# More q, k and x transposes by DMA, loads moved up, and a last output tile of 384 + 128 columns

## The chip, the cores and the metric

The kernel runs on one core of one Trainium2 chip. Time is device time in microseconds (us) for one execution; lower is better. Each kernel was run several times, alternating with the kernel before on the same chip. Most executions of a kernel agree well; a run over 1.5% above the fastest of the same kernel is called slow and left out of the ratios, though not of the medians.

Ratios are the mean time of one kernel's fast runs over the mean of the other's fast runs in the same rounds, so they are not quite the ratios of the medians that stand beside them. Where I turn a difference of ratios into microseconds I multiply by 249.3.

## The reference

Sliding-window attention with four sink keys, then a gated feed-forward layer on its output:

```python
scores = q @ k.T / sqrt(64)                     # 4 batches, 8 heads, 768 positions
keep   = (key position < 4) | (0 <= rel < 128)  # four sinks, a window of 128
a      = softmax(where(keep, scores, -1e9))
x      = (a @ v), heads side by side            # 3072 tokens x 512
xn     = x / sqrt(mean(x * x) + 1e-6) * rms_g
g      = xn @ w_gate                            # 512 x 1536
out    = (g * sigmoid(g) * (xn @ w_val)) @ w_out
```

## The kernel before

The 3072 tokens are 24 blocks of 128: `g = 6 b + t`, batch `b`, block `t` of the batch. Four blocks make a feed-forward group of 512 columns, so there are six groups, G = 0 to 5. Attention of later blocks is laid into the "slots" between the feed-forward parts of earlier groups.

A block's q and k are loaded as bf16 with the tokens on the partitions, and must be transposed before scores can be taken. The kernel does this on TensorE up to block 13 and for block 18, else by DMA on SyncE's queue:

```python
DMA_T_FROM = 14          # q, k: from this block by DMA
DMA_X_FROM = 12          # x: the same

def by_dma(g):
    return g >= DMA_T_FROM and g % NT > 0          # NT = 6: not the first block of a batch

def unit_t(g):
    ...
    if by_dma(g):
        for i, src in enumerate((QS.pop(g), KS_.pop(g))):
            nc.sync.dma_start_transpose(out=QKT[b][:, i, :, t * P:(t + 1) * P], in_=...)
        return
    ps = psum.tile(...)                            # 8 transposes on TensorE,
    transposes(ps, QS.pop(g), 0)
    transposes(ps, KS_.pop(g), HP * P)
    nc.scalar.copy(out=QKT[b]..., in_=ps...)       # and one copy by ScalarE
```

The four sink keys of a batch are the first four columns of its first block's k. They are copied out once per batch, by two small copies on ScalarE:

```python
def unit_sink(b):
    ks = sink.tile([P, HP * KSW], BF16, name="ksk")
    ...
    for hi in range(2):
        nc.scalar.copy(out=ksv[pr, :, hi * NS:(hi + 1) * NS], in_=QKT[b][pr, 1, :, 0:NS])
    ...
```

GpSimd issues the loads and, from block 8 on, also masks the exponentials. Output tiles go through three buffers (`opool`, bufs=3), copied out of PSUM by ScalarE and stored from SyncE's queue:

```python
slots:  step(g) puts unit_s(g), unit_attend(g - 1), unit_t(g + 2 or g + 3), unit_sink, two loads
LOADS = [(14, 15), (16, 17), (18, 19), (20, 21), (22, 23)]     # one pair per step, from g = 9
```

All PSUM tiles are one bank each and take eight banks in turn.

The softmax here doesn't subtract the row's maximum and nothing guards it: scores larger than these inputs give would overflow.

## Time and profile before

| | before |
|---|---|
| median of three runs | 249.14 us (249.09 to 249.48) |
| span of the profiled run | 248.5 us |
| TensorE busy, granted clock | 241.8 us, 1.00 |
| q, k transposes on TensorE | 15 blocks of 24 |
| x transposes on TensorE | 12 blocks of 24 |
| DMA engines | full for 19 of 40 slices, until about 118 us, then mostly idle |

TensorE is the bound: a kernel can only be shorter if TensorE does less, or waits less at the two ends. The lines that show it are in the prediction. Some words used there and below: the chain is the sequence of instructions and transfers that ended last, followed back from the last instruction; the pitch is the time from one instruction's start to the next one's. Tile names: `pqk` and `pxt` are transposes on TensorE, `qkT` and `xnt` the transposed q, k and x; `pT` are scores, `et` their exponentials, `pv` their products with v; `pg` and `pvl` are the gate and value matmuls, `th` the tanh of the gate, `p` and `hT` what VectorE makes of them; `po` is the output matmul and `osb` its copy.

### The profile page before, as it was taken

What the parts mean: (1) busy time and instruction counts of PE and PEld (TensorE: products, weight loads), DVE (VectorE), ACT (ScalarE), POOL (GpSimd) and SP (SyncE); (2) the same over time, 40 slices, a digit from 0 to 9 for tenths busy, and PEclk for the clock granted to TensorE, in tenths of its full rate; (3) what the DMA queues carried; (4) which work ended last, traced back from release to release, by engine and by line L of the source; (5) the groups of instructions that cost most, each with busy time, mean ns of one, the idle gap of its engine ahead of it and who ended that gap; (6) DMA issues with size and microseconds to landing.
All of it is one profiled execution on the core that took longest, in us unless ns stands there. A gap on an engine that the chain in (4) does not pass through costs nothing.

```text
span 248.5 us, 4926 instructions
## 1 busy us (share of the span) xinstructions
PE 241.8 (97%) x1850; PEld 129.5 (52%) x1850; DVE 163.6 (66%) x368; ACT 145.2 (58%) x336; POOL 105.1 (42%) x141
## 2 busy tenths in 40 slices
PE   7999999999999999999999999999999999999994
PEld 2566887856445554544454454444444444444443
DVE  5465896878467789339778368769167885387700
ACT  2779657898977774874674375674475242333221
POOL 8977676496398995970331000233231000000000
PEclk9999999999999999999999999999999999999999
DMA  9999999999959999599000694001610003500022
GB/s 128 153 171 192 190 160 187 183 155 188 126 69 144 148 129 161 91 161 164 0 3 12 158 168 88 0 4 22 190 46 0 3 0 63 190 3 0 0 86 84
DMA packets 102873, 24.96 MB, mean 100 GB/s; under 512 B 91841, under 2 KB 99905, under 8 KB 102850
## 3 DMA queue, kind: packets, MB, share of 16 engines
q0 software_dynamic: 80704, 13.90, 73.4%
q1 hardware_dynamic: 20962, 10.43, 18.4%
q10 hardware_dynamic: 1184, 0.33, 0.6%
q8 instruction: 14, 0.23, 0.4%
q14 instruction: 9, 0.07, 0.1%
HBM read 28.31 MB, written 6.29 MB: 139 GB/s over the span
## 4 chain that ended last, share of the span: by engine, by line
PE 90%; ACT 4%; DVE 2%; DMA 2%; issue 0%; ACTq 0%
PE pg L642 25%; PE pvl L642 25%; PE po L712 22%; PE pT L411 4%; PE pv L467 3%; PE pqk L245 2%; PE pv L471 2%; DMA osb<-in_q_dram 2%; ACT et L420 2%; PE pw L332 1%; PE po L684 1%; PE pT L342 1%; PE pv L453 1%; ACT sq L519 1%; PE pT L357 1%; PE pxt L612 1%
## 5 line engine op out<-in xcount | busy, mean ns | idle before, releaser
L642 PE MATMUL pg<-xnt,wg 128*128 128x512 bf16 (+1 forms) x336 | 74.2, 348 | 0.2 <-ACT xnt L630 0.2
L642 PE MATMUL pvl<-xnt,wv 128*128 128x512 bf16 (+1 forms) x336 | 74.0, 349 | 0.0
L660 DVE SCALAR_TENSOR_TENSOR p<-th,pg 128x512 bf16<-128x512 bf16 x72 | 49.3, 684 | 28.4 <-ACT th L655 28.0
L655 ACT ACTIVATE th<-pg 128x512 bf16<-128x512 f32 x72 | 43.3, 604 | 41.8 <-PE pg L642 40.6
L712 PE MATMUL po<-wo,hT 128*128 128x512 bf16 x276 | 63.2, 379 | 0.0
L670 DVE TENSOR_TENSOR hT<-p,pvl 128x512 bf16<-128x512 bf16 x72 | 49.5, 687 | 7.8 <-PE pvl L642 1.1
L388 POOL TENSOR_SCALAR_AFFINE_SELECT et<-et 128x512 bf16<-128x512 bf16 x28 | 19.0, 684 | 73.3 <-ACT et L420 73.3
L642 PEld LDWEIGHTS <-wv 128*128 128x128 bf16 x336 | 32.4, 98 | 29.6 <-issue 0.2
L642 PEld LDWEIGHTS <-wg 128*128 128x128 bf16 x336 | 31.4, 98 | 26.1 <-issue 1.0
L420 ACT ACTIVATE et<-pT 128x512 bf16<-128x512 f32 x76 | 39.5, 610 | 3.7 <-PE pT L411 3.6
L712 PEld LDWEIGHTS <-hT 128*128 128x128 bf16 x276 | 26.1, 98 | 28.8 <-issue 0.2
L719 ACT ACTIVATE osb<-po 128x512 f32<-128x512 f32 x23 | 13.8, 599 | 30.9 <-PE po L712 27.4
L519 ACT ACTIVATE sq<-x 128x256 bf16<-128x256 bf16 x48 | 20.4, 429 | 8.9 <-DVE x L508 8.5
L121 POOL DMA_DIRECT2D v<-in_v_dram x24 | 21.9, 913 | 3.8 <-DMA wo<-in_moe_w_out_dram 2.0
L108 POOL DMA_DIRECT2D qs<-in_q_dram x23 | 21.0, 911 | 4.7 <-DMA wo<-in_moe_w_out_dram 3.0
L108 POOL DMA_DIRECT2D ks<-in_k_dram x23 | 20.9, 907 | 1.9 <-issue 0.7
L503 DVE RECIPROCAL rden<-pv 128x4 f32<-128x4 f32 x48 | 7.5, 172 | 21.5 <-PE pv L471 21.3
L508 DVE TENSOR_TENSOR x<-pv,rden 128x256 bf16<-128x256 f32 x48 | 19.8, 422 | 1.0
L582 DVE SCALAR_TENSOR_TENSOR xr<-x,y,gb 128x512 bf16<-128x512 bf16 x22 | 16.9, 816 | 0.3
L393 POOL TENSOR_SCALAR_AFFINE_SELECT et<-et 128x512 bf16<-128x512 bf16 x22 | 14.8, 673 | 0.0
L471 PE MATMUL pv<-v,et 128*128 128x65 bf16 x168 | 12.6, 194 | 0.1
L411 PE MATMUL pT<-qkT 64*128 64x256 bf16 (+1 forms) x168 | 12.3, 262 | 0.2 <-ACT et L420 0.2
(83 smaller groups left out, 198.8 us busy)
## 6 DMA issues: line engine op xcount, KB each, us to landing
out_dram<-osb SPq DMA_DIRECT2D x23, 256.0 KB, 2.5
v<-in_v_dram POOLq DMA_DIRECT2D x24, 128.0 KB, 6.8
qs<-in_q_dram POOLq DMA_DIRECT2D x23, 128.0 KB, 6.4
ks<-in_k_dram POOLq DMA_DIRECT2D x23, 128.0 KB, 6.7
wg<-in_moe_w_gate_dram POOLq DMA_DIRECT2D x6, 256.0 KB, 8.1
wv<-in_moe_w_val_dram POOLq DMA_DIRECT2D x6, 256.0 KB, 8.4
wo<-in_moe_w_out_dram POOLq DMA_DIRECT2D x2, 768.0 KB, 10.4
osb<-in_k_dram ACTq DMA_DIRECT2D x1, 256.0 KB, 4.9
```

What stands on the lines that cost most here:

```text
L108: nc.gpsimd.dma_start(out=tl, in_=src[b, :, t * P:(t + 1) * P, :].rearrange("h t d -> t h d"),)
L121: nc.gpsimd.dma_start(out=V16[b][:, t, :, 0:D], in_=v[b, :, t * P:(t + 1) * P, :].rearrange("h t d -> t h d"),)
L388: nc.gpsimd.affine_select(out=ev[:, :, 0, :], in_=ev[:, :, 0, :], compare_op=ALU.is_ge, fill=0.0, base=0, pattern=[[0, x], [1, P]], channe ...
L411: nc.tensor.matmul(out=banks[u][hi][:, j * w:(j + 1) * w], lhsT=QKT[b][pr, 1, hp, t * P:(t + 1) * P], rhs=QKT[b][pr, 0, hp, t * P:t * P + ...
L420: nc.scalar.activation(out=et[:, hi].rearrange("p j n c -> p (j n c)"), in_=banks[u][hi], func=ACT.Exp, scale=inv_sqrt_d,)
L508: nc.vector.tensor_tensor(out=X16[g][:, heads_of(g, u), :], in0=pvv[:, :, 0:D], in1=RDEN.pop((g, u)).unsqueeze(2).to_broadcast((P, 4, D)), ...
L519: nc.scalar.activation(out=sq, in_=xh, func=ACT.Square, scale=MS_SCALE, accum_out=MS[g - i][:, i, u:u + 1],)
L642: nc.tensor.matmul(out=ps[:, i * n:(i + 1) * n], lhsT=w_sb[:, kt, ft * P:(ft + 1) * P], rhs=XNT[G][:, kt, cols], start=(kt == 0), stop=(kt ...
L655: nc.scalar.activation(out=st["th"], in_=st["pg"], func=ACT.Tanh, scale=0.5)
L660: nc.vector.scalar_tensor_tensor(out=p1, in0=st["th"], scalar=1.0, in1=st["pg"], op0=ALU.add, op1=ALU.mult,)
L670: LAST[0] = nc.vector.tensor_tensor(out=HT[key][:, i:i + n, cols], in0=p1.rearrange("p (n c) -> p n c", n=n), in1=pvl.rearrange("p (n c) - ...
L712: nc.tensor.matmul(out=st["po"], lhsT=HT[(G, ft // 2)][:, ft % 2, tb * P:(tb + 1) * P], rhs=wo[:, ft, :], start=(ft == 0), stop=(ft == FTN ...
```

## The change

Its intent: take transposes from TensorE, the bound, and give them to DMA; load two blocks earlier so that their data is there; and shorten the tail by one copy.

```diff
-    DMA_T_FROM = 14
-    DMA_X_FROM = 12
+    DMA_T_FROM = 10
+    DMA_X_FROM = 8
...
     def by_dma(g):
-        return g >= DMA_T_FROM and g % NT > 0
+        return g >= DMA_T_FROM
...
     def parts_last(G, tb):
-        (two halves of 256 columns; the second copied as 128 + 128 by ScalarE and VectorE)
+        def cols(c):
+            lo, hi = ((0, 3 * P), (3 * P, DM))[c]
+            (12 matmuls on columns lo:hi)
+            nc.scalar.mul(osb, po[:, 0:hi - lo], 0.5)
+            (nc.sync, nc.scalar)[c].dma_start(out=out[row:row + P, lo:hi], in_=osb)
...
-        if g + 2 < NB and not by_dma(g + 2):
-            slots[4].append(lambda: unit_t(g + 2))
-        if g + 3 < NB and by_dma(g + 3):
+        if 14 <= g + 3 < NB:
             slots[4].append(lambda: unit_t(g + 3))
...
-    LOADS = [(14, 15), (16, 17), ...]
+    LOADS = [(), (16, 17), ...]
...
-        (21, lambda: unit_t(10)),
+        (18, lambda: unit_t(10)),
+        (20, lambda: unit_t(11)),
+        (22, lambda: unit_t(12)),
+        (24, lambda: unit_t(13)),
...
-        for g in range(2 * GB + 2, 2 * GB + 6):
+        for g in range(2 * GB + 2, 2 * GB + 8):
             FIRST.append((3 * g - 28, lambda g=g: unit_load(g)))
```

More of the change, by code (lines that the diff above doesn't have):

```diff
@@ L678, in parts_last @@
     def parts_last(G, tb):
-        def half(c):
+        def cols(c):
             po = psum.tile([P, 512], FP32, name="po", tag="b1")
-            n = DM // 2
+            lo, hi = ((0, 3 * P), (3 * P, DM))[c]
             for ft in range(FTN):
                 nc.tensor.matmul(
-                    out=po[:, 0:n], lhsT=HT[(G, ft // 2)][:, ft % 2, tb * P:(tb + 1) * P],
-                    rhs=wo[:, ft, c * n:(c + 1) * n], start=(ft == 0), stop=(ft == FTN - 1),
+                    out=po[:, 0:hi - lo], lhsT=HT[(G, ft // 2)][:, ft % 2, tb * P:(tb + 1) * P],
+                    rhs=wo[:, ft, lo:hi], start=(ft == 0), stop=(ft == FTN - 1),
                 )
             row = (G * GB + tb) * P
-            for i in range(1 + c):
-                m = n // (1 + c)
-                osb = opool.tile([P, m], FP32, name=f"ol{c}{i}", bufs=1)
-                if i:
-                    nc.vector.tensor_scalar(
-                        out=osb, in0=po[:, i * m:(i + 1) * m], scalar1=0.5, scalar2=None,
-                        op0=ALU.mult,
-                    )
-                else:
-                    nc.scalar.mul(osb, po[:, 0:m], 0.5)
-                (nc.sync, nc.scalar)[c - i].dma_start(
-                    out=out[row:row + P, c * n + i * m:c * n + (i + 1) * m], in_=osb,
-                )
-        return [lambda: half(0), lambda: half(1)]
+            osb = opool.tile([P, hi - lo], FP32, name=f"ol{c}", bufs=1)
+            nc.scalar.mul(osb, po[:, 0:hi - lo], 0.5)
+            (nc.sync, nc.scalar)[c].dma_start(out=out[row:row + P, lo:hi], in_=osb)
+        return [lambda: cols(0), lambda: cols(1)]
     def parts_o(G, tb):
@@ L746 @@
     AT = [(0, 8, 14, 20, 28), (0, 10, 18, 27)]
-    LOADS = [(14, 15), (16, 17), (18, 19), (20, 21), (22, 23)]
+    LOADS = [(), (16, 17), (18, 19), (20, 21), (22, 23)]
     def run(parts, slots):
```

## The prediction

> **What bounds the kernel now.** I read the head of the page first (busy shares, the forty slices), then the chain that ended last, then the waits of TensorE, and only then single stretches of time.
>
> ```profile
> PE 241.8 (97%) x1850; PEld 129.5 (52%) x1850; DVE 163.6 (66%) x368; ACT 145.2 (58%) x336; POOL 105.1 (42%) x141
> ...
> PEclk9999999999999999999999999999999999999999
> DMA  9999999999959999599000694001610003500022
> ...
> PE 90%; ACT 4%; DVE 2%; DMA 2%; issue 0%; ACTq 0%
> ```
>
> TensorE is busy 241.8 of 248.5 us at full clock, and 90% of the chain lies on it. Its busy time by stretches shows where the other 6.7 us lie: 2.2 in the first 20 us, 0.2 in the next 20, 0.5 between 60 and 70 us, and 3.75 after its last matmul; elsewhere it is never idle. All its waits on other engines are these:
>
> ```profile
> PE pw L332 <- DVE idle L99: 1.3, 1, 1.3
> PE pqk L245 <- DVE qs L190: 0.6, 1, 0.6
> PE pT L411 <- ACT et L420: 0.2, 1, 0.2
> PE pg L642 <- ACT xnt L630: 0.2, 1, 0.2
> PE pv L453 <- ACT xnt L621: 0.2, 1, 0.2
> ```
>
> So from 17 us to 245 us an instruction taken from TensorE shortens the kernel by its pitch, unless what replaces it comes late. The second thing to see is the DMA row: the engines are full for the first 18 slices (to about 112 us) but for two, and the added transposes for blocks 8 to 15 fall into that part. The third is GpSimd, whose program order holds both the loads and the masks; between 49 and 68 us it goes like this (timeline of GpSimd; start, length, idle before in brackets):
>
> ```profile
> 42.49 0.88 POOL L121 DMA_DIRECT2D v<-in_v_dram  x1 [1.97 <-DMA wo<-in_moe_w_out_dram]
> ...
> 49.15 0.87 POOL L108 DMA_DIRECT2D qs<-in_q_dram  x1 [3.02 <-DMA wo<-in_moe_w_out_dram]
> ...
> 59.05 0.92 POOL L121 DMA_DIRECT2D v<-in_v_dram  x1
> 66.04 0.63 POOL L388 TENSOR_SCALAR_AFFINE_SELECT et<-et 128x512 bf16<-128x512 bf16 x1 [6.07 <-ACT et L420]
> ```
>
> The two bracketed waits both end when the load issued eight places earlier lands (the two halves of the output weights, issued at 32.86 and 37.05 us, landing 9.3 and 11.5 us later); the waits between 16 and 22 us fit the same count. So no more than eight loads of this queue are outstanding. From 49 us the loads go out every 0.88 us and land 6.4 to 7.5 us later: eight times 0.88 is 7.0, so they run just under that limit. The 6.07 us gap before the first mask is the only free time there.
>
> **What the Trainium skill says.** "TensorE: Matmul & The Clock Gate", section "Part 4: PE-mode transpose", gives about 275 ns for a 128x128 bf16 transpose in a kernel, and says that the result goes to PSUM and needs a copy. The trace's records say 219 ns, but in a row only the pitch counts: eight q and k transposes take 0.45 us of the chain, 56 ns each. I use the trace. "DMA: Bandwidth & Descriptors", section "Queues, rings and completion order", says that each DMA engine takes turns between queues packet by packet. The trace agrees in kind: a transpose lands in 2.4 us with quiet DMAs and in 6.2 to 8.8 us between 102 and 110 us, where loads run beside it. "ScalarE: Activation LUTs", section "What ACT_TABLE_LOAD costs", gives 186 ns + 0.833 ns per column for an operation with immediate scale; the trace has 383 ns for 256 columns and 277 for 128, so agreeing within some 20 ns. "PSUM — Partial Sum Buffer", section "PSUM bank collisions raise a hardware error", says that two engines may not read one bank at once and get ordered. That fits the tail: VectorE begins its copy at 245.10, when ScalarE's ends.
>
> ```profile
> 241.97 2.78 PE L684 MATMUL po<-wo,hT 128*128 128x256 bf16 x24
> ...
> 244.79 0.28 ACT L698 ACTIVATE ol<-po 128x128 f32<-128x128 f32 x1 [0.93 <-PE po L684]
> 245.09 0.36 ACTq L699 DMA_DIRECT2D out_dram<-ol  x1
> 245.10 0.29 DVE L693 TENSOR_SCALAR ol<-po 128x128 f32<-128x128 f32 x1 [9.46 <-ACT ol L698]
> ```
>
> **The change part by part.**
>
> *q and k.* Blocks 10, 11, 12, 13 and 18 leave TensorE (9 blocks went by DMA, 14 will). Each costs the chain 8 transposes x 56 ns = 0.45 us. 5 x 0.45 = 2.2 us, all on the bounding engine.
>
> *x.* Blocks 8 to 11 leave it too: 4 transposes each, 4 x 56 ns = 0.22 us; 4 x 0.22 = 0.9 us.
>
> *Copies out of PSUM.* ScalarE loses 5 copies of 1.01 us and 4 of 0.61 us, 7.5 us together, nearly all beside other work. The exception is the stretch of 56 to 68 us, where the chain leaves TensorE for ScalarE: there TensorE waits 0.2 us for an exponential and 0.2 us for a copy. Block 10's copy (1.00 us at 63.71) stands just ahead of these exponentials, so I count these waits as gone: 0.4 us.
>
> *Tail.* The matmuls stay as long: now 2.63 us for 24 of 256 columns; then 12 of 384 columns, 12 x 0.75 x 216 ns = 1.94 us (216 ns is 10.36 us over 48 matmuls of 512 columns) and 12 of 128 columns at the 56 ns pitch of the transposes = 0.67 us, sum 2.61. The copy of 384 columns (about 0.49 us, between 383 ns for 256 and 600 for 512) starts when its bank is complete and fits into the 0.67 us of the second part. Then the last copy starts as ScalarE's does now, and its store is issued at about 245.09 on ScalarE's own queue instead of 245.41 on SyncE's: 0.3 us earlier. The earlier store is larger (192 KB instead of 128), so some of this may be lost; I count 0.2 us.
>
> *Loads.* Blocks 14 and 15 (six loads, 6 x 0.88 = 5.3 us of GpSimd) move from 71.3-76.6 us to behind block 13, that is from 60 us into the 6.07 us gap. In itself nothing.
>
> Sum of what is saved: 2.2 + 0.9 + 0.4 + 0.2 = 3.7 us, 1.5%.
>
> **The rivals: waits that take the place of what is removed.**
>
> *First, around 66 us.* Three things meet in the first group's end. (a) The scores of block 9 need q of block 10, now by DMA. SyncE's order puts it behind the second output store, which goes out at 58.65; with a landing of 6 to 9 us it arrives at 65 to 68 us, and TensorE wants it at about 65.3. (b) GpSimd's six loads just fit the gap, but only if they are not held by the limit of eight. With landing times as now the last goes out at about 66.4; block 10 and 11's transposes take DMA time (I estimate 0.85 us each beside loads: 13.2 us of DMA work from 104.5 to 117.7 held six loads at 0.88, three stores at about 0.9, and six transposes), which makes it 67 to 68. (c) The masks of block 8 follow the loads in order, and its attention, which now runs at 67.67, needs the third mask, 1.8 us after the first begins. It would end near 70 instead of 68.1, though TensorE could be there at 66.9. Against it: the landing times may be shorter, since half a DMA engine's turns do not mean half of its bytes. No stall here: 0; a full one: 3 us. I take 1.0.
>
> *Second, around 106 us.* x of blocks 8 to 11 goes by SyncE in front of the output stores of that group. VectorE delivers them at 98.4 to 100.7; four issues at 1.2 us end at 103.5, in traffic (up to 2.3 us each, as at 107.68) at about 105. The stores wait behind them, and the fourth output copy needs the buffer of the first (three buffers). Its PSUM bank is the one that the next group's first gate matmul gets, eight allocations later. For it: late in the kernel ScalarE waits 2.5 us for just such a store already. Against it: at 135 us the same order costs nothing, because the DMAs are quiet; there the four x go from 135.07 to 140.2, the store lands before 143.25. At 106 us the loads of blocks 22 and 23 come in the way. None to 4 us; I take 0.7.
>
> *Third, nothing stalls:* 249.1 - 3.7 = 245.4. *Both stall in full:* 245.4 + 7 = about 252; the sum of two worst cases, unlikely.
>
> **Range and chances.** 249.14 - 3.7 + 1.0 + 0.7 = 247.1; I say 247.0. The low end is the unhindered 245.4 less 0.7 for pitch and waits that I undersize: 244.7. The high end is one full stall and a bit of the other, 249.6. Over 2% faster means under 244.2, more than the whole sum: 0.07. Over 2% slower means over 254, beyond both full stalls: 0.03. Within 2%: 0.90.
>
> **What would show it.** Right: 40 transposes of pqk and 16 of pxt fewer; the chain still on TensorE by nine tenths; the last store issued 0.3 us after the last matmul ends; TensorE's busy time lower by about 3 us. First rival: TensorE idle just before the attention of block 8 or the scores of block 9, the first mask later than 66 us, brackets naming a load at GpSimd's issues. Second rival: idle before the first gate matmul of the third group, with ScalarE waiting for an output store there. I would be wrong below if TensorE's removed work also freed a weight load or a PSUM bank that I count as hidden, and wrong above if the transposes slow every load to 112 us so that later blocks come late too.

## More of the kernel before

The order of TensorE, SyncE and GpSimd is the program's ("manual"); ScalarE's is left to the scheduler of the build from the first group on, VectorE's from that group's second half on.

One more view belongs here, since the prediction did not look at it: ScalarE's timeline where the sink keys of the third batch (block 12) are copied. Columns are start, length, engine and line, operation, output from input, and in brackets how long the engine had been idle and what ended that.

```profile
81.08 1.01 ACT L279 COPY qkT<-pqk 128x1024 bf16<-128x1024 bf16 x1 [0.65 <-PE pqk L245]
82.00 0.60 ACT L655 ACTIVATE th<-pg 128x512 bf16<-128x512 f32 x1
82.50 0.40 ACT L290 COPY ksk<-qkT 64x16 bf16<-64x16 bf16 x2
```

ScalarE itself writes the transposed block at 81.08 us and reads the sink keys out of it at 82.50 (`ksk`). What the second needs was made on the same engine just before it, so it cannot wait.

## The result, and the profile after

| | before | changed |
|---|---|---|
| median | 249.25 us (249.09 to 249.48, 4 runs) | 262.12 us (261.31 to 262.75, 4 runs) |
| ratio of the fast runs | | 1.0514, interval 1.0482 to 1.0545 |
| span of the profiled run | 248.5 us | 260.6 us |
| granted clock of TensorE | 1.00 | 0.974 |

The kernel is 5% slower, outside the predicted range and in the direction given 3 in 100. The head of the page of the changed kernel, to set against the first fence of the prediction:

```profile
PE 245.4 (94%) x1794; PEld 128.2 (49%) x1794; DVE 163.2 (63%) x367; ACT 139.5 (54%) x327; POOL 105.3 (40%) x141
...
PEclk9999999999779999999679999999999999999999
DMA  9999999999999999999000066300350001610012
...
PE 78%; DMA 8%; DVE 5%; ACT 4%; POOL 3%; issue 1%; SPq 0%; DVEq 0%; ACTq 0%; POOLq 0%
```

The 56 transposes have gone (1794 matmuls, not 1850), yet TensorE is busy 3.6 us longer: the clock row has two dents, at 65 to 78 us and at 124 to 137 us, and matmuls take twice as long there. The last line is the share of each engine in the chain: DMA has entered it with 8% (it had 2%). TensorE's longest waits on other engines:

```profile
PE pT L411 <- DVE p L660: 3.3, 1, 3.3
PE pg L642 <- ACT osb L709: 2.2, 1, 2.2
PE pv L471 <- POOL et L388: 2.1, 2, 1.5
PE pT L411 <- ACT osb L709: 1.3, 1, 1.3
```

Of these the second is the prediction's second rival, and the third and fourth are its first. (The fourth stands before the scores of block 9 and is put down to ScalarE's `osb`; the same wait in experiments 1, 5 and 6 is put down to `qkT<-qs`, block 10's q, as foreseen.) The 3.3 us for VectorE's `p` is new. VectorE's `p` waits for ScalarE's tanh (`th`), so ScalarE's timeline tells what held it:

```profile
75.40 0.20 ACT L290 COPY ksk<-qkT 64x16 bf16<-64x16 bf16 x1 [4.87 <-DMA qkT<-ks]
75.51 0.58 ACT L655 ACTIVATE th<-pg 128x512 bf16<-128x512 f32 x1
...
112.37 0.60 ACT L709 ACTIVATE osb<-po 128x512 f32<-128x512 f32 x1 [4.70 <-DMA out_dram<-osb]
...
123.58 0.42 ACT L290 COPY ksk<-qkT 64x16 bf16<-64x16 bf16 x2 [6.62 <-DMA qkT<-ks]
124.02 1.58 ACT L655 ACTIVATE th<-pg 128x512 bf16<-128x512 f32 x3
```

Twice ScalarE stands still for a sink-key copy of 0.2 us whose input is now a DMA transpose: the k of block 12 and, at 123.58, of block 18. The tanh behind it had its matmuls long before.

The two waits did not cost the same. During the first, TensorE still had matmuls in front of it: it was busy without a gap from 70.2 to 80 us (at half its clock until 74.9, see below), and it then waited 0.33 us for `p`. During the second it ran dry:

```profile
81.03 0.27 PE L453 MATMUL pv<-vsk,esk 64*128 64x260 bf16 x1 [0.33 <-DVE p L660]
...
125.39 0.27 PE L411 MATMUL pT<-qkT 64*128 64x256 bf16 x1 [3.26 <-DVE p L660]
```

The Trainium skill, page "PSUM — Partial Sum Buffer", section "Engine vs sequencer instructions", says that ScalarE's queue is strict FIFO; here three tanh are done at once as soon as the copy is through, at 124.02. The order of ScalarE's instructions in the two builds shows why the copy stands where it does. In the kernel before it comes after block 12's copy from PSUM, as it must. In the changed kernel nothing on ScalarE comes before it, and the build has put it ahead of the second group's first tanh:

```text
before                                     changed
sq   (block 8)                             sq   (block 8)
th                                         ksk  (first half)
sq   (block 8)                             th
th, copy of block 11, th, th               sq   (block 8)
...                                        ksk  (second half)
th, copy of block 12, th                   th, th, th
ksk, ksk                                   ...
```

The program itself asks for the sink keys only at the end of that group (slot 30 of 36). With block 18 it is the same: its copy stood behind the third group's last tanh (131.51 us), and now stands behind the second; the program asks for it in the fourth group. The builds of before and of experiment 1, with the producer on ScalarE, have the copy behind it; without the producer it stands far ahead. Why the scheduler picks that place, no run shows. The chain of the changed kernel runs over both transposes (start, length, what):

```profile
67.48 7.89 DMA qkT<-ks
...
118.46 5.10 DMA qkT<-ks
```

And the clock. Busy time of each engine in stretches of 2 us, with the granted clock in the third column from the right, then DMA share and GB/s:

```profile
66.00:68.00 2.00, 0.86 (x11) 0.50 (x11) 0.00 (x0) 1.57 (x4) 1.02 (x3) 1.00 2.17 139
68.00:70.00 2.00, 0.77 (x11) 0.62 (x12) 0.61 (x2) 0.79 (x2) 2.00 (x4) 0.52 1.97 146
70.00:72.00 2.00, 2.00 (x12) 0.90 (x11) 0.61 (x2) 0.51 (x2) 2.00 (x4) 0.50 1.48 192
...
124.00:126.00 2.00, 0.27 (x1) 0.09 (x1) 1.24 (x2) 1.98 (x5) 0.00 (x0) 1.00 0.00 0
126.00:128.00 2.00, 1.39 (x8) 0.36 (x8) 1.90 (x4) 1.66 (x4) 1.35 (x3) 0.52 0.00 0
```

The clock is halved from 68.1 to 74.9 us and from 126.1 to 132.9 us, 6.8 us each; four matmuls of 512 columns take 1.71 us of the chain there, not 0.86. The first halving begins before ScalarE's first wait for a transpose (70.5 us): it follows TensorE's waits at 66 us. The second follows the sink-key copy of block 18. The skill's page "TensorE: Matmul & The Clock Gate", section "Part 1: The HAM clock gate (the "warmup" mystery)", says that an idle TensorE falls to half its clock after about 3.4 us, and needs about as long of work to get it back. The factor agrees; the idle time doesn't quite, see the last section. In the last two lines the DMAs do nothing, so traffic is not what slows the second stall's end.

GpSimd between 59 and 68 us, against the third fence of the prediction:

```profile
63.91 0.88 POOL L108 DMA_DIRECT2D qs<-in_q_dram  x1 [0.74 <-DVE y L564]
65.25 0.88 POOL L108 DMA_DIRECT2D ks<-in_k_dram  x1 [0.46 <-PE pxt L612]
67.10 0.88 POOL L121 DMA_DIRECT2D v<-in_v_dram  x1 [0.97 <-DMA qs<-in_q_dram]
67.98 0.65 POOL L388 TENSOR_SCALAR_AFFINE_SELECT et<-et 128x512 bf16<-128x512 bf16 x1
```

The six moved loads no longer fit in the gap: the first mask begins at 67.98 us, not 66.04 (the prediction's "67 to 68"). The releasers named in the brackets of the first two lines had nothing to do with a load; the last names one.

The tail:

```profile
257.53 0.28 ACT L690 ACTIVATE ol<-po 128x128 f32<-128x128 f32 x1 [0.18 <-PE po L684]
257.84 0.36 ACTq L691 DMA_DIRECT2D out_dram<-ol  x1
```

The last matmul ends at 257.50, the last store is issued 0.34 us later; before it was 0.65.

**The theories.** A: ScalarE's order. The sink-key copies of blocks 12 and 18, placed early by the build, wait for DMA transposes and hold every tanh behind them; with the clock that falls after the second. B: the traffic. The added transposes make every load, mask and transpose late, and the copy's wait is only one face of it. C: the first rival of the prediction (loads in front of masks, block 10's q) and the second (x in front of output stores), larger than I sized them. To tell them apart I moved only the copy, only the transposes, only the loads, or only a buffer.

### The profile page after: what moved, and what is told of

It reads as the page before. It is cut to its first block, busy times and chain, and to the rows that moved or that the text cites. A ratio compares the mean times of both kernels' runs of the same rounds, so it can differ in the third digit from the quotient of the medians.

```text
span 260.6 us, 4843 instructions
## 1 busy us (share of the span) xinstructions
PE 245.4 (94%) x1794; PEld 128.2 (49%) x1794; DVE 163.2 (63%) x367; ACT 139.5 (54%) x327; POOL 105.3 (40%) x141
## 4 chain that ended last, share of the span: by engine, by line
PE 78%; DMA 8%; DVE 5%; ACT 4%; POOL 3%; issue 1%; SPq 0%; DVEq 0%; ACTq 0%; POOLq 0%
PE pg L642 22%; PE pvl L642 21%; PE po L702 18%; DMA qkT<-ks 5%; PE pT L411 3%; DMA v<-in_v_dram 3%; PE pw L332 3%; PE pv L467 2%; PE pv L471 2%; ACT et L420 2%; DVE hT L670 2%; PE pqk L245 2%; DVE p L660 1%; PE po L684 1%; PE pT L342 1%
## 5 line engine op out<-in xcount | busy, mean ns | idle before, releaser
L642 PE MATMUL pg<-xnt,wg 128*128 128x512 bf16 (+1 forms) x336 | 76.9, 358 | 2.4 <-ACT osb L709 2.2
L642 PE MATMUL pvl<-xnt,wv 128*128 128x512 bf16 (+1 forms) x336 | 75.8, 355 | 0.0
L655 ACT ACTIVATE th<-pg 128x512 bf16<-128x512 f32 x72 | 42.7, 600 | 44.8 <-PE pg L642 43.6
L702 PE MATMUL po<-wo,hT 128*128 128x512 bf16 x276 | 62.5, 379 | 0.0
L642 PEld LDWEIGHTS <-wg 128*128 128x128 bf16 x336 | 32.4, 100 | 31.1 <-issue 6.5
L471 PE MATMUL pv<-v,et 128*128 128x65 bf16 x168 | 13.5, 198 | 2.2 <-POOL et L388 2.1
```

Of the source, the lines that this page charges most:

```text
L642: nc.tensor.matmul(out=ps[:, i * n:(i + 1) * n], lhsT=w_sb[:, kt, ft * P:(ft + 1) * P], rhs=XNT[G][:, kt, cols], start=(kt == 0), stop=(kt ...
L655: nc.scalar.activation(out=st["th"], in_=st["pg"], func=ACT.Tanh, scale=0.5)
L702: nc.tensor.matmul(out=st["po"], lhsT=HT[(G, ft // 2)][:, ft % 2, tb * P:(tb + 1) * P], rhs=wo[:, ft, :], start=(ft == 0), stop=(ft == FTN ...
```

## The experiments

**1. Blocks 12 and 18 on TensorE again.**

```diff
-        return g >= DMA_T_FROM
+        return g >= DMA_T_FROM and g % NT > 0
     (and unit_t(12), unit_t(18) at the slots that they had before)
```

> The changed kernel, but the first blocks of the last two batches (12 and 18) are transposed on TensorE again, at the places they had before; nine q,k blocks fewer things change: 10, 11, 13, the x blocks, the moved loads and the tail stay. Theory A (ScalarE's order): the copies of the sink keys out of blocks 12 and 18 stand in ScalarE's queue ahead of the first tanh of the groups and wait there 4.87 and 6.62 us for a DMA transpose. From the first gate matmul to the first output matmul the second group took 27.74 us instead of 25.96 although 1.35 us of transposes had left it, the third 31.50 instead of 24.04 although 0.45 had: 3.1 + 7.9 = 11.0 us. A expects these back less two blocks of 0.45 us: 262.1 - 11.0 + 0.9 = 252.0 us, granted clock 1.00, no wait of ScalarE for a transpose. Theory B (too much DMA traffic, loads and masks late): 4 of 26 transposes less change little, 259 us or more.

Measured: 252.76 us, ratio 1.0159 (1.0132 to 1.0185). That is A's number within 0.8 us. ScalarE no longer waits for a transpose. B, which asked for 259 or more, is out as the main cause, but the transposes of two blocks left the DMAs too, so experiments 2 and 5 keep all of the traffic.

**2. The sink-key copies on GpSimd.**

```diff
-            nc.scalar.copy(
+            (nc.gpsimd.tensor_copy if b >= 2 else nc.scalar.copy)(
```

> The changed kernel with every transpose by DMA at the same place and nothing else moved, but the sink-key copies of the last two batches (four copies of 64x16) on GpSimd instead of ScalarE, in GpSimd's fixed order, where they stand just before their first use. Same traffic, only the queue that waits is another. Theory A: 262.1 - 11.0 = 251.1 us, less up to 1 us of GpSimd's slower copies; no wait of ScalarE for a transpose. Theory B (traffic): 260 to 262. If B is right about part, the time falls between and the rest of the idle time of TensorE stays in the same places.

Measured: 255.96 us, ratio 1.0273 (1.0233 to 1.0312). Between the two. Part of the remainder was made by the experiment: TensorE waits 2.5 us for the copy, which on GpSimd stands behind six loads. The rest is where the first rival was expected (1.6 us for block 10's q, 2.5 us for masks) and in ScalarE's 4.6 us wait for an output store.

**3. x of blocks 8 to 11 on TensorE again** (`DMA_X_FROM = 12`).

> The changed kernel with x of blocks 8 to 11 on TensorE again (the second rival of the prediction undone by itself). That rival: TensorE's 2.17 us wait of the first gate matmul of the third group for an output copy goes, and 0.9 us of transposes comes back; ScalarE's 4.70 us wait for a store goes. Theory A says that this leaves the 11 us of the sink-key copies: 261 us, within 1.5 us of the changed kernel. If the x transposes in front of the stores were what starts the large stall (the clock falls after it), the time would fall below 256.

Measured: 259.5 us, ratio 1.0414 (1.0377 to 1.0451), 2.5 us less than the changed kernel where I had expected 1. The large stall stays (ScalarE waits 10.1 us for two transposes of k). So x by DMA costs 2.5 us net here, 3.4 with the 0.9 us of transposes that came back, and is not what starts the rest.

**4. The new tail alone, on the kernel before.**

> The kernel before with the change of the last output tile alone. The prediction's working: last store issued 0.3 us earlier, of which 0.2 is counted: 249.05 us, ratio 0.999. From the two profiles the time from the last matmul's end to the end of the span fell from 3.74 to 3.1 us, which would be 0.6 us: 248.6. If the larger first store holds the second back: no gain, 249.2.

Measured: 249.08 us, ratio 1.000 (0.9985 to 1.0015). No gain that can be told from none; more than 0.4 us is excluded.

**5. The copies on ScalarE, but later.** The one experiment that changes nothing but the order of one engine: the build is told to place these copies after the latest tanh of the program.

```diff
+            if b >= 2:
+                with tc.issue_after(LASTA[0]):      # the last tanh issued so far
+                    copy()
```

> The changed kernel with all its transposes by DMA and its sink-key copies on ScalarE, but the build is told to put these copies behind the tanh that comes before them in the program, so that they stand at the end of the second and third group's tanhs instead of at their beginning. One order on one engine differs from the changed kernel. Theory A (ScalarE's order): the 4.87 and 6.62 us waits of ScalarE for a transpose go; what stays is what stayed when GpSimd did these copies (255.96 us), so 255.5, between 254.5 and 256.5. If not the order but the engine or the traffic counted, it stays at 260 to 262.

Measured: 254.64 us, ratio 1.0202 (1.0166 to 1.0237); 7.8 us less than the changed kernel, with every transpose where it was. The repeat on another chip (experiment 12) gave 1.0141, 9.3 us less. ScalarE's waits for a DMA, all of them, now read

```profile
ACT osb L716 <- DMA out_dram<-osb: 6.9, 2, 4.4
```

and none is for a transpose. In the trace the copies now stand here:

```profile
98.00 0.40 ACT L290 COPY ksk<-qkT 64x16 bf16<-64x16 bf16 x2
...
161.21 0.41 ACT L290 COPY ksk<-qkT 64x16 bf16<-64x16 bf16 x2
```

Apart from them, the instructions of ScalarE, VectorE and GpSimd come in the same order as in the changed kernel's trace. This shows A: where four copies of 0.2 us stand in ScalarE's queue costs 8 to 9 us.

Which of the two waits was it? From its first gate matmul to its first output matmul, the third group took 31.34 us in the changed kernel and 23.43 in experiments 5 and 12; the second group took 27.58, 25.57 and 27.19. So most of it, 7.9 us, is block 18's copy alone: TensorE's waits of 3.3, 0.5 and 0.4 us there, and 6.8 us at half clock, which are about 3.4 us more (an estimate), make 7.6. Block 12's copy costs at most some 2 us, within what the stall at 66 us scatters.

**6. Experiment 1 with the loads of 14 and 15 where they were.**

> The kernel of the first experiment (first blocks of batches on TensorE, 252.76 us) with the loads of blocks 14 and 15 where they were before. Theory C (first rival of the prediction, the part with GpSimd): its waits in front of block 8's attention, 1.6 us behind a load that GpSimd could not issue and 0.7 us for the mask, go, because no load stands before the masks: 250.5 us; and if the clock stays at full speed because the idle time falls from about 3.8 to 1.5 us, another 1.5 to 1.8: 249.0. If the loads moved up are harmless: 252.5.

Measured: 249.21 us, ratio 1.000 (0.9953 to 1.0046), as expected. The waits for masks and behind GpSimd's loads are gone; TensorE's wait for block 10's q stays, 2.4 us now, and it alone was enough to halve the clock from 67.4 to 70.8 us. (The profile fell on the slowest of four runs, 250.98 us; two others, at 248.7, had a clock of 0.998 and 1.000.)

**7. Also block 10 on TensorE, and a fourth output buffer.**

```diff
-    DMA_T_FROM = 10
+    DMA_T_FROM = 11
-    opool = ctx.enter_context(tc.tile_pool(name="opool", bufs=3))
+    opool = ctx.enter_context(tc.tile_pool(name="opool", bufs=4))
```

> The sixth with block 10 on TensorE as before as well (no wait for its q at 66 us) and a fourth output buffer (no wait for an output store at 106 us). Transposes of 11, 13 and of x 8 to 11 stay by DMA, with the new tail. The sum of the prediction without any new wait: 249.1 - 2 x 0.45 - 0.9 = 247.3 us, ratio 0.993. If some other wait takes their place: 249 or more.

Measured: 247.47 us, ratio 0.9914 (0.9886 to 0.9941), clock 1.00. Faster than both kernels. TensorE's waits are those of the kernel before again:

```profile
PE pw L332 <- DVE idle L99: 1.3, 1, 1.3
PE pg L642 <- ACT xnt L630: 0.3, 1, 0.3
PE pT L411 <- ACT et L420: 0.2, 1, 0.2
PE pv L453 <- ACT xnt L621: 0.2, 1, 0.2
```

**8. Dummy matmuls in TensorE's waits.** Experiment 1 with six matmuls on zeros ahead of block 9's scores and seven behind.

> The kernel of the first experiment with 13 dummy matmuls of 128x512 (2.8 us at full clock) laid into TensorE's two waits before and after the scores of block 9, where it stands idle about 3.8 us. Theory D (an idle TensorE loses its clock for some us after): the matmuls after it run at full speed, which gives back about 1.8 us (four matmuls take 1.4 to 1.7 us instead of 0.86): 251.0 us, granted clock 1.00. If the clock falls for another reason: 252.8, or up to 2.8 us more where the dummies do not fit into the waits.

Measured: 251.66 us, ratio 1.0073 (1.0027 to 1.012), that is 2.1 us below experiment 1 by ratio, 1.1 by median (two chips). The two kernels between 70 and 72 us, experiment 1 first:

```profile
70.00:72.00 2.00, 1.74 (x10) 0.97 (x12) 0.61 (x2) 0.51 (x2) 2.00 (x4) 0.50 1.41 284
```

```profile
70.00:72.00 2.00, 0.88 (x17) 0.65 (x18) 0.65 (x3) 0.47 (x2) 2.00 (x4) 1.00 1.69 183
```

With work that is good for nothing the clock stays at 1.00 although TensorE still waits 2.0 us for masks. So it is TensorE's idleness that halves the clock, and in experiment 1, where the clock was halved for 3.4 us, this costs 1 to 2 us on top of the stall.

**9. The seventh with three buffers.**

> The seventh (candidate, 247.47 us) with three output buffers again, so it is the sixth with block 10 alone put back on TensorE. Two questions in one: against the sixth (249.21) it shows what block 10's q by DMA costs, expected 2.4 us of wait and about 0.5 us of slowed clock less 0.45 us of transposes, so 246.8 to 247.3 without the buffer; against the seventh it shows the fourth buffer: the second rival's wait was 0.7 us of TensorE in the sixth's profile (first gate matmul for an output copy). Together: 247.9, between 247.4 and 248.3. If the fourth buffer does nothing, 247.4; if it is the larger part, 249.

Measured: 248.2 us, ratio 0.9955 (0.9939 to 0.997), as expected. Against the sixth it is block 10's q: 1.1 us. Against the seventh it is the buffer: 1.0 us. (Each pair ran on two chips; each ratio is against the kernel before on its own.)

**10. The fifth with a fourth buffer.**

> The fifth (sink copies behind the tanh, everything else as the changed kernel; 254.64 us) with a fourth output buffer. The second rival of the prediction alone: ScalarE's 4.4 us wait for an output store and TensorE's 1.9 us wait for that output copy go: 252.7 us. If another wait ends at the same time there (the x transposes landing late): 254 or more.

Measured: 250.56 us, ratio 1.005 (1.0024 to 1.0077), 2 us less than expected. ScalarE's wait for a store and TensorE's for the output copy are gone, but the profiles also differ by 2.1 us at the first gate matmul of the second group (72.44 us in the fifth, 70.32 here), where ScalarE waits for no output store in either trace. Experiments 12 and 13 repeat the pair.

**11. All of it but block 10:** late sink copies, loads where they were, block 10 on TensorE, four buffers; blocks 11, 12, 13 and 18 and x of 8 to 11 by DMA.

> Sink copies behind the tanh, loads of 14 and 15 where they were, block 10 on TensorE, four output buffers: blocks 11, 12, 13 and 18 and x of 8 to 11 by DMA. The prediction's sum without the waits that it or I found since: 249.2 - 4 x 0.45 - 0.9 = 246.5 us, ratio 0.989; 0.9 us under the seventh. If the sink blocks by DMA still cost a wait somewhere: 247.5 or more.

Measured: 246.59 us, ratio 0.9882 (0.9866 to 0.9899), the expected number within 0.1 us, and the fastest kernel: 0.8 us under the seventh by ratio. Blocks 12 and 18 by DMA are a gain once nothing waits for their sink keys.

**12 and 13. The fifth and the tenth again, on one chip.**

> The fifth kernel again, unchanged (254.64 us). Beside the next run on the same chip. If chips or runs differ in the stall around 66 us, it moves by a microsecond or two; otherwise 254.6 within 0.7.

> The tenth kernel again (250.56 us), on the same chip as its partner with three buffers. If the buffer's part is the wait it removes: 1 to 2 us under the partner, and the rest of the 4.1 was chip or timing. If it is really 4 us on one chip too: the buffer changes more than that wait.

Measured: 253.85 us (ratio 1.0141, 1.0107 to 1.0174; one run at 256.79 was slow and is left out of the ratio) and 251.55 us (1.0073, 1.0046 to 1.01). The buffer is worth 1.7 us, the wait that it removes. The rest of the 4.1 us was not the buffer: in kernels that still stall at 66 us, that stall differs by a microsecond or two between runs and chips.

**14. The changed kernel with four buffers.**

> The changed kernel (262.12 us) with a fourth output buffer and nothing else. If the waits add up: 262.1 less the 2.2 us of TensorE's wait for the output copy = 260. If the wait for the sink-key copy that follows absorbs it (its k of block 18 lands when it lands): 261.5 to 262.

Measured: 261.07 us, ratio 1.0467 (1.0419 to 1.0514), 1.2 us less. The intervals overlap, so I claim no more than a tendency. In its profile TensorE's wait behind VectorE's `p` has grown from 3.3 to 4.9 us: part of what the buffer saves is waited for at the next stall, the sink-key copy.

**15. The eleventh with the loads moved up.**

> The eleventh (246.59 us) with the loads of 14 and 15 moved up as in the changed kernel, block 10 on TensorE. First rival, the part of loads in front of masks: GpSimd's six loads are held by the limit of eight, the masks of block 8 come late, TensorE waits 1.5 to 2.5 us[...]: 248.5 to 250. If only block 10's transpose made the loads late: 246.6 to 247.2.

Measured: 248.99 us, ratio 0.996 (0.9924 to 0.9997; one run at 251.31 was slow and is left out of the ratio). The moved loads alone cost 1.9 us, and they make the time scatter: 247.41 to 249.09 in the fast runs, clock 0.991 to 0.998, where the eleventh kept within 246.39 to 246.99. The profile fell on the quickest run, in which TensorE waits only 0.7 us for a mask.

**What the 13 us are made of,** as differences of ratios along experiments 5 (and 12), 10 (and 13), 15 and 11: the changed kernel 1.0514; sink copies later, 1.0202 and 1.0141, so 8 to 9 us; a fourth buffer, 1.005 and 1.0073 (1.7 us on one chip); block 10 on TensorE (experiment 15), 0.996, so 2.2 to 2.8 us; loads back, 0.9882, 1.9 us. The last gives a kernel that keeps 0.9 + 1.8 us of the change's gains.

## Why the prediction was wrong

It was wrong in direction and size: 247.0 in 244.7 to 249.6, measured 262.12.

**The step that failed: the list of what the transposed blocks feed.** "5 x 0.45 = 2.2 us, all on the bounding engine" counted blocks 12 and 18 like the others, and the rivals asked only for scores and attention. But the diff strikes out `g % NT > 0`, and these two blocks have a second reader, the sink-key copy on ScalarE. The two changes that did it together: the copy's input became a DMA of 5 to 8 us beside loads, and with no producer left on ScalarE the build moved the copy forward, in the second group from behind the seventh tanh to ahead of the first, in the third from behind the last to behind the second. Neither was in the prediction; it cost 8 to 9 us (experiments 5 and 12), 7.9 of it in the third group behind block 18's k, against 0.9 us of transposes saved for these two blocks. "Both stall in full: 252" was called unlikely; without this third stall the changed kernel is at 253.9 to 254.6.

**First rival: mechanism right, size wrong.** Taken at 1.0 us, at most 3. Each of its parts came: the q of block 10 late, the six loads held, the mask at 67.98. Together the two parts are 1.9 us for the loads and 2.2 to 2.8 for block 10 while the loads are moved (1.1 when they are not), net of the 0.45 us that block 10 saves. Two things were missing. The stall at 66 us is long enough to halve the clock, 1 to 2 us more (experiment 8), and I had counted no clock at all. And a chance of one third of a full stall was too hopeful here: the loads were said to "run just under that limit", but of the landings given, 6.4 to 7.5 us, some lie above 7.0, and the working itself had the last load out at 66.4 us or later, behind the first mask's 66.04.

**Second rival: mechanism right, size low.** Taken at 0.7 us, measured 1.7 on one chip (12 against 13), within the 0 to 4 that it was given; experiment 3, which took the x transposes themselves away, found 3.4 before the 0.9 us that they save. The chain was as told: x transposes, then the stores, then the buffer, then the bank of the first gate matmul.

**The gains were right.** Experiment 11 keeps 4 x 0.45 + 0.9 us of them and comes out at 246.59, where this sum gives 246.5. The part of the working that turned chain pitches into time held. One reading was off, and nothing rests on it: the DMA row is full for 19 slices, to 118 us, not 18.

**ScalarE's 0.4 us: not shown.** The waits before block 9's scores were still there in experiments 7 and 11, but in both block 10's copy was back on ScalarE, so they do not test it.

**Tail: 0.2 us expected, none found** (experiment 4). The copies took the predicted lengths (0.49 and 0.28 us) and the store went out 0.3 us earlier, but the time didn't follow within 0.4 us. Why is open. The profiled run of before was one of the longer ones (250.16 us in all), with its first cast on VectorE at 0.88 us where the fourth experiment's took 0.43, so tails of single profiles are compared with care.

## What to carry to other kernels

When an operation moves to another engine or to DMA, list every reader of its result, not only the obvious one; a guard in the old code (`g % NT > 0`) can be a hint of such a reader. Where a scheduler orders an engine, a producer on that engine also pins its readers' place: take it away, and a tiny copy can come to stand ahead of the engine's main work and wait there for a DMA. Size a stall of TensorE by its wait plus the slow matmuls after it, and distrust a plan whose loads only just fit into a gap.

## What the Trainium skill lacked or had wrong

- "TensorE: Matmul & The Clock Gate", section "Part 1: The HAM clock gate (the "warmup" mystery)": it gives about 3.4 us of idle time for the fall of the clock. The factor of two agrees (1.71 against 0.86 us for four matmuls), but in experiment 6 a wait of 2.4 us with 0.2 us just before it was enough, and in the changed kernel a wait of 1.3 us and the first 0.9 us of the next, with 0.9 us of work between, before the clock fell at 68.1. The page does say that its window runs freely; these numbers show that shorter waits are enough. The halved stretches lasted 6.8 us in the changed kernel and 3.4 in experiments 1 and 6.
- The same page, section "Part 4: PE-mode transpose": about 275 ns for a 128x128 transpose in a kernel. In a row only the pitch counts, and that was 56 ns here (0.45 us for eight); the page has no pitch for transposes.
- "Advanced Engine Details and Errata", section "X-Bar Transpose (TRN2)": it calls transposes by DMA as fast as regular DMAs. A 128x512 bf16 transpose of x (128 KB) landed in 2.4 us with quiet DMAs, a plain store of 128 KB in 1.7 (another direction, so a rough comparison); one of q or k beside loads took 5 to 9 us, and no page has a figure for that.
- No page has the limit of eight outstanding loads on GpSimd's queue, which the waits of the kernel before show (the load waits for the one eight places earlier). Whether the chip or the build sets it, no run here tells.
